# First queries of an attention + MoE kernel: order of loads, place of phi, and a mark for the second-layer weights

## The chip, the cores and the metric

One core of a Trainium2 chip. The metric is the device time of one execution in microseconds (us); lower is better.

## What is computed

Four batches of 576 tokens, 8 heads of 64. Causal attention is mixed with a read from a memory matrix, and the result goes through two matrix products with a gate between them:

```python
scores = where(causal, -1e9, q @ k.T / sqrt(D))
a = exp(scores - scores.max(-1)); a /= a.sum(-1) + 1e-09
local = a @ v
q_p = where(q > 0, q, exp(q) - 1) + 1            # phi
mem_out = (q_p @ M_prev) / (q_p . z_prev + 1e-06)
x = g * mem_out + (1 - g) * local                # g = sigmoid(beta)
h = x @ w_in                                     # 2304 x 512 by 512 x 2048
out = (h * sigmoid(1.702 * h)) @ w_out           # 2048 x 512
```

The weights arrive as 64-bit floating point and are rebuilt on the chip as 32-bit words.

## The kernel before

The work is tiled by pairs of heads: 4 batches times 4 pairs (`NP`) are 16 pairs, numbered 0 to 15. Tokens of a pair stand in blocks of 128 rows. A product with split operands (`mm` into `pm`) uses a high and a low part of each factor.

**First queries.** `first_queries(0)` computes the first 256 queries of batch 0, for all four pairs, before the planned part begins, so that the first tokens of x are there early. It loads the keys and queries of each pair (`fk`, L261 and L262, two loads each), the queries in rows (`fq`, L265), z (`fz`, L267), the values (`fv`, L269) and the memory (`fm`, L271), all on SP's queue. Then it goes through `score(c)` (products of L286 into a pair of PSUM tiles; VectorE masks and takes the maximum, L479, in place; ScalarE exponentiates, L485), `norm(c)` (sums, scaling, transposes L304 to L306, and the copies into `ft`, on ScalarE L136 and on VectorE L139), `phi` (Relu L314 and Exp L315 on ScalarE, then VectorE L316 and products with z on VectorE and GpSimd, and the scaling of the memory by ScalarE), `phin` (sums L325, reciprocal, scaling), `qtr(k)` (transposes of the queries, L339) and `values(c)` (L350), which adds memory and local part of a pair and splits the result into `xh` and `xl`. PSUM tiles come from `bank`, which hands out four tiles in turn.

**w_in.** 16 blocks of 128 columns. `conv_unit` loads a block of 64-bit words (`wraw`, 512 KB, L198 on SP's queue), ScalarE scales the upper words (`ws`, L206), VectorE puts the 32-bit word together in three steps (L213, L214, L216), ScalarE copies its high part and GpSimd subtracts to get the low part (`wi`). Two buffers for raw words serve the first six blocks (`W0`); later odd blocks have two of their own. The first six are written out behind `first_queries`, the others at the slots in `CONV`.

**Pairs.** `plan_prep` and `plan_attend` lay out the 16 pairs in numbered slots (`K0`, `at`), `first_moe` fills TensorE's remaining time with the first product of x, chunk by chunk (256 or 320 tokens of batch 0, 288 of the others). At the start of a pair's slots stands its tail: the last 64 rows of both heads, with `exp_tail` (ScalarE, tile `at`). Outputs of the pairs of a batch go out to memory (`xd<-xf`, L646) and come back as `xl` (L640 or L708). The first product's results are copied (`hk`) and stored (`gd`), to be loaded again for the second product.

**w_out.** `conv_pair(kk)` loads two blocks of raw words of the second-layer weights on GpSimd's queue (`load`, L847), then ScalarE (L851) and VectorE rebuild them. The calls stand behind the sixteen pairs in the program text. Where their buffers are free at the start, nothing in the program keeps the loads from being taken much earlier.

**Order.** Each engine works through its own list in order. The list is made by the framework: of the instructions whose inputs are there in its own plan, it takes the one that stands first in the program text (`tc.high_priority` moves a group ahead). `tc.add_manual_dep(x, y, NOSYNC)` only says that x comes behind y in that list; with `SYNC` the engine of x also waits for y. SP and GpSimd issue DMAs from their lists like any other instruction. The call order in `first_queries` is:

```python
score(0); phi(); score(1); norm(0); phin(); score(2); norm(1)
qtr(0); qtr(1); values(0, xl); score(3); norm(2)
values(1, xl); norm(3); values(2, xl); values(3, xl)
```

Of the kernel before, what the change touches and what calls it, by code (L numbers as in the profile page):

```python
# [16 lines left out]
NP = H // 2  # L17
# [17 lines left out]
def tile_attention_memory_moe(ctx, tc, kq, vq, mem, zz, beta, w_in, w_out, out):  # L35
# [157 lines left out]
    def conv_unit(slot, dst, src, rp, rkw, wp, wkw, sp, skw):  # L193
# [7 lines left out]
        def scale():  # L201
            if wp() is None:
                box["s"] = box["r"] = sp.tile([128, DM], F32, name="wr", **skw)
            else:
                box["s"] = wp().tile([128, DM], F32, name="ws", **wkw)
            nc.scalar.activation(  # L206
                out=box["s"], in_=box["raw"][:, :, 1].bitcast(F32), func=AF.Copy, scale=2.0 ** -112)

# [13 lines left out]
        if slot is None:  # L222
            for fn in parts:
                fn()
            return
# [26 lines left out]

    direct, done = set(), set()

    def first_queries(b):
# [3 lines left out]
        for c in range(NP):  # L259
# [3 lines left out]
            K.append(t)  # L263
        q = fst.tile([128, NP, 2, 128], F32, name="fq")
        nc.sync.dma_start(q, vq[b, :, :, 1, :2].rearrange("c p t d -> p c t d"))  # L265
        z = fst.tile([128, NP, 128], F32, name="fz")
        nc.sync.dma_start(z.rearrange("p c d -> p (c d)"), zz[b:b + 1].rearrange("o c d -> o (c d)").to_broadcast([128, NP * 128]))  # L267
        v = fst.tile([128, NP, 2, 128], F32, name="fv")
        nc.sync.dma_start(v, vq[b, :, :, 0, :2].rearrange("c p t d -> p c t d"))  # L269
        m = fst.tile([128, NP, 128], F32, name="fm")  # L270
        nc.sync.dma_start(m, mem[b * NP:b * NP + NP].rearrange("c p h d -> p c (h d)"))  # L271
# [9 lines left out]
        def score(c):  # L281
# [7 lines left out]
            for h in range(2):  # L289
                for i, (o, n) in enumerate(((256, 128), (0, 256))):  # L290
                    nm = softmax_max([(ps[h][:, o:o + n], n, mask[:, 512 - n:])])
                    softmax_exp(ps[h][:, o:o + n], aa[c][:, h, o:o + n], nm, fsm[c][:, h, i, :1])

        def norm(c):
# [13 lines left out]
            copy("A", fa[c][:, :512], pt[0])  # L308
            copy("V", fa[c][:, 512:], pt[1][:, :256])

        def phi():
            qv = q.rearrange("p c t (h d) -> p (c t) h d", h=2)
            w = qm[:, :, :, :D]
            nc.scalar.activation(out=w, in_=qv, func=AF.Relu, scale=-1.0)  # L314
            nc.scalar.activation(out=w, in_=w, func=AF.Exp, scale=-1.0)  # L315
            nc.vector.scalar_tensor_tensor(out=qv, in0=qv, scalar=0.0, in1=w, op0=ALU.max, op1=ALU.add)  # L316
            for c in range(NP):
                tt("VP"[c % 2], w[:, 2 * c:2 * c + 2], qv[:, 2 * c:2 * c + 2],
                   z[:, c:c + 1, :].rearrange("p o (h d) -> p o h d", h=2).to_broadcast([128, 2, 2, D]), ALU.mult)
                copy("A", m[:, c], m[:, c], gt[:, c:c + 1])  # L320
# [38 lines left out]
        phi()  # L359
        score(1)  # L360
        norm(0)
        phin()
        score(2)
        norm(1)
        qtr(0)
        qtr(1)
        values(0, xl)
        score(3)
# [4 lines left out]
        values(3, xl)  # L373

# [115 lines left out]
    def plan_attend(p):  # L490
# [63 lines left out]
        def exp_tail():  # L554
            U["at"] = wkp.tile([128, S], F32, name="at", bufs=2)
            U["st"] = tails[p % 2]
            for f in range(2):
                x = softmax_exp(U["ps"][f][:, :CH], U["at"][:, CH * f:CH * f + CH], U["nm"], U["st"][:, f:f + 1])
                used(U["ps"][f], x)

# [214 lines left out]

    def conv_in(blk):
        wb[blk] = w1[blk].tile([128, 2, DM], F32R, name=f"wi{blk}")
        other = blk >= W0 and blk % 2 == 1
        raw = (att, {"tag": "W1", "bufs": 2}) if other else (cnv, {"bufs": 2})
        ws = (lambda: ps_o, {"tag": "po"}) if other else (lambda: ps_x, {"tag": "ps"})  # L780
# [291 lines left out]
```

## Time and profile before

| | us |
|---|---|
| median of three runs | 641.17 |
| lowest and highest run | 640.54, 646.22 |
| profiled execution, its own time | 648.07 |
| span of the profiled execution (first to last instruction) | 646.3 |
| TensorE busy in the span | 602.6 |

The profile is of one execution. Its span is the time from the first to the last instruction. A row of a timeline gives start, duration, engine, line, operation and tiles, then in brackets how long the engine stood idle before and what released it ("<-"). Stretches give the busy time of each engine in a window with the number of instructions, the granted TensorE clock (1.00 is full speed), the mean share of the DMA engines and what they moved. The chain of waits is followed back from the last instruction: each piece is what ended last.

### The profile page before, as it was taken

Reading aid. Unit: us, or ns where it says so; the run is one execution under the profiler, and the core shown is the slowest. Engines: PE = TensorE matmul, PEld = TensorE weight load, DVE = VectorE, ACT = ScalarE, POOL = GpSimd, SP = SyncE. Lnnn points to the kernel's source line nnn. Section 1 sums busy time; section 2 is a strip of 40 time slices with the busy share of each in tenths; the row PEclk is TensorE's granted clock in tenths of the full one; section 3 lists DMA queues with packets and bytes.
Section 4 is the critical chain, followed back from the end, with each engine's and each line's share of the span. In section 5 each row is a group of like instructions: output and inputs, shape, how many; then the busy total and the mean of one; then the engine's idle time right before and its main releaser. Section 6 shows DMA issues by size and latency. Waiting matters only on the chain.

```text
span 646.3 us, 11501 instructions
## 1 busy us (share of the span) xinstructions
PE 602.6 (93%) x4000; PEld 522.7 (81%) x4000; DVE 414.3 (64%) x1015; ACT 363.0 (56%) x836; POOL 183.7 (28%) x253
## 2 busy tenths in 40 slices
PE   3698998999979999989999999899989999999997
PEld 2458765688657787778888889899989999999996
DVE  3998866654665445544455437889496579458944
ACT  4776575544564468354554335665876764776451
POOL 3556644532456433343544112310000000000000
PEclk9988999999999999999999999899999999999999
DMA  8848642323444155243342115775745630671002
GB/s 248 297 148 261 186 158 88 129 70 129 138 134 138 52 177 167 73 153 96 123 153 83 49 66 186 231 238 173 238 145 171 186 133 15 206 212 57 25 2 73
DMA packets 59370, 90.61 MB, mean 140 GB/s; under 512 B 5680, under 2 KB 48176, under 8 KB 59312
## 3 DMA queue, kind: packets, MB, share of 16 engines
q1 hardware_dynamic: 57008, 81.49, 40.1%
q0 software_dynamic: 2304, 8.39, 4.2%
q8 instruction: 31, 0.51, 0.3%
q14 instruction: 27, 0.22, 0.1%
HBM read 63.02 MB, written 26.84 MB: 139 GB/s over the span
## 4 chain that ended last, share of the span: by engine, by line
PE 66%; DMA 12%; ACT 9%; DVE 7%; issue 3%; SPq 1%; POOL 1%; DVEq 0%; ACTq 0%; POOLq 0%
PE acc L935 23%; PE pm L125 22%; PE po L125 7%; PE pt L131 7%; PE ps L125 7%; DMA gd<-hk 3%; DMA xl<-xd 3%; DMA xd<-xf 2%; DMA g<-gd 2%; ACT a L485 2%; DMA fq<-in_vq_dram 1%; DVE g L144 1%; ACT hk L136 1%; DMA qr<-in_vq_dram 1%; DVE ps L479 1%
## 5 line engine op out<-in xcount | busy, mean ns | idle before, releaser
L125 PE MATMUL pm<-xh,wi 128*128 128x288 f32 (+2 forms) x1024 | 219.4, 307 | 11.3 <-ACT hk L136 5.9
L125 PEld LDWEIGHTS pm<-xh,wi 128*128 128x128 f32 x1024 | 168.5, 194 | 14.9 <-ACT hk L136 7.0
L935 PE MATMUL acc<-oh,wo 128*128 128x384 f32 x672 | 158.3, 337 | 0.9 <-ACT oh L136 0.7
L125 PE MATMUL pm<-xl,wi 128*128 128x288 f32 (+2 forms) x512 | 154.3, 303 | 0.0
L935 PEld LDWEIGHTS acc<-oh,wo 128*128 128x128 f32 x672 | 120.0, 188 | 2.7 <-ACT oh L136 2.7
L144 DVE TENSOR_TENSOR ol<-g,oh 128x768 fp32r<-128x768 f32 x84 | 79.2, 955 | 49.0 <-ACT oh L136 44.4
L479 DVE CUSTOM_DVE_ANT_0 ps<-ps,mask 128x256 f32<-128x256 f32 (+4 forms) x144 | 67.5, 506 | 61.6 <-PE ps L125 54.8
L488 POOL TENSOR_SCALAR a<-a,sm,g 128x512 f32<-128x512 f32 (+3 forms) x112 | 71.6, 651 | 116.4 <-DVE sm L538 100.0
L935 PE MATMUL acc<-ol,wo 128*128 128x384 f32 x336 | 99.7, 339 | 2.7 <-DVE ol L144 2.6
L125 PEld LDWEIGHTS pm<-xl,wi 128*128 128x128 f32 x512 | 98.6, 193 | 1.1 <-DVE wr L216 1.1
L485 ACT ACTIVATE a<-ps,nm 128x256 f32<-128x256 f32 (+2 forms) x112 | 59.9, 542 | 63.9 <-DVE nm L479 63.1
L136 ACT ACTIVATE oh<-g 128x768 fp32r<-128x768 f32 x84 | 70.2, 840 | 42.3 <-PE acc L935 40.9
L125 PE MATMUL ps<-kqf 128*128 128x288 f32 (+4 forms) x288 | 67.9, 480 | 4.6 <-ACT at L485 2.3
L935 PEld LDWEIGHTS acc<-ol,wo 128*128 128x128 f32 x336 | 61.5, 188 | 5.3 <-DVE ol L144 5.3
L136 ACT ACTIVATE hk<-pm 128x288 f32<-128x288 f32 (+2 forms) x85 | 34.1, 410 | 38.2 <-PE pm L125 26.8
L131 PE MATMUL pt<-ident,a 128*128 128x128 f32 x296 | 53.2, 274 | 0.0
L898 ACT ACTIVATE g<-g 128x768 f32<-128x768 f32 x48 | 40.3, 844 | 20.3 <-DMA g<-gd 17.8
L125 PEld LDWEIGHTS po<-e,vr 128*64 128x64 f32 x416 | 29.9, 137 | 20.1
L131 PE MATMUL pt<-ident,at 128*128 128x128 f32 x160 | 41.4, 285 | 4.9 <-ACT a L485 3.5
L125 PE MATMUL po<-e,vr 128*64 128x320 f32 (+3 forms) x416 | 45.4, 359 | 0.0
L144 DVE TENSOR_TENSOR g<-g,g 128x768 f32<-128x768 f32 x48 | 44.1, 953 | 1.2 <-ACT g L898 1.1
L125 PEld LDWEIGHTS ps<-kqf 64*128 64x128 f32 (+1 forms) x288 | 30.1, 189 | 17.8 <-issue 7.4
(127 smaller groups left out, 751.5 us busy)
## 6 DMA issues: line engine op xcount, KB each, us to landing
g<-gd SPq DMA_DIRECT2D x48, 384.0 KB, 3.9
gd<-hk SPq DMA_DIRECT2D x96, 144.0 KB, 2.0
wraw<-in_w_out_dram POOLq DMA_DIRECT2D x16, 512.0 KB, 4.8
wraw<-in_w_in_dram SPq DMA_DIRECT2D x16, 512.0 KB, 4.8
kqf<-in_kq_dram SPq DMA_DIRECT2D x12, 608.0 KB, 6.6
vr<-in_vq_dram SPq DMA_DIRECT2D x16, 320.0 KB, 6.0
qr<-in_vq_dram SPq DMA_DIRECT2D x12, 320.0 KB, 3.2
xd<-xf SPq DMA_DIRECT2D x10, 288.0 KB, 6.4
```

Source lines behind the costliest of these rows:

```text
L125: x = nc.tensor.matmul(out, l, r, start=start, stop=stop)
L131: nc.tensor.transpose(out, in_, idn)
L136: return nc.scalar.activation(out=dst, in_=src, func=AF.Copy, **kw)
L144: (nc.vector if eng == "V" else nc.gpsimd).tensor_tensor(out=dst, in0=a, in1=b, op=op)
L479: nc.vector.tensor_tensor_reduce(out=ps, in0=ps, in1=mk, op0=ALU.add, op1=ALU.min, scale=-0.125, scalar=1e38 if j == 0 else nm[:, j - 1:j] ...
L485: return nc.scalar.activation(out=a, in_=ps, func=AF.Exp, scale=-1.0, bias=nm, accum_out=sm)
L488: (nc.vector if eng == "V" else nc.gpsimd).tensor_scalar(out=a, in0=a, scalar1=r, scalar2=gcol, op0=ALU.mult, op1=ALU.mult)
L898: nc.scalar.activation(out=t, in_=t, func=AF.Gelu_apprx_sigmoid)
L935: nc.tensor.matmul(acc[b, j][:, :QN], W[2 * p + kk][:, WPART[i], sp, 128 * j:128 * j + 128], mv[:, kk], start=first and p + kk == 0 and sp ...
```

## The change

In `first_queries` the loads go out as fk of pairs 0 and 1, fq, fk of pairs 2 and 3, fz, the raw words of w_in block 0, fm, fv. `phi` is called behind `norm(1)`, its Relu behind the ScalarE copy of `ft` of pair 0; the scaling of the memory stands behind the copy of `ft` of pair 1. `score(3)` is called ahead of `qtr` and `values`. The first scaling of w_in words stands behind the last exponential of `score(2)`. All these are orders of ScalarE's list, without a wait. The loads of w_out wait for the last exponential of the tail of the thirteenth pair (number 12). `conv_unit` hands back its five parts, so that the first load can be issued apart from the rest.

```diff
@@ -203,8 +203,11 @@
                 box["s"] = box["r"] = sp.tile([128, DM], F32, name="wr", **skw)
             else:
                 box["s"] = wp().tile([128, DM], F32, name="ws", **wkw)
-            nc.scalar.activation(
+            x = nc.scalar.activation(
                 out=box["s"], in_=box["raw"][:, :, 1].bitcast(F32), func=AF.Copy, scale=2.0 ** -112)
+            behind = state.pop("behind", None)
+            if behind is not None:
+                tc.add_manual_dep(x.ins, behind, NOSYNC, reason="raw words")
 
         def bits():
             raw, si = box["raw"], box["s"].bitcast(I32)
@@ -220,9 +223,7 @@
         parts = (load, scale, bits, lambda: copy("A", dst[:, 0], box["r"]),
                  lambda: sub("P", dst[:, 1], box["r"], dst[:, 0]))
         if slot is None:
-            for fn in parts:
-                fn()
-            return
+            return parts
         for k, prio, fn in zip((0, 2, 2, 3, 3), (5, 60, 61, 40, 41), parts):
             at(slot + k, prio, fn)
 
@@ -250,25 +251,41 @@
         copy("A", xh[:, c, :w], src)
         sub("V", xl[:, c, :w], src, xh[:, c, :w])
 
+
+    def conv_in(blk):
+        wb[blk] = w1[blk].tile([128, 2, DM], F32R, name=f"wi{blk}")
+        other = blk >= W0 and blk % 2 == 1
+        raw = (att, {"tag": "W1", "bufs": 2}) if other else (cnv, {"bufs": 2})
+        ws = (lambda: ps_o, {"tag": "po"}) if other else (lambda: ps_x, {"tag": "ps"})
+        return conv_unit(None, wb[blk], w_in[blk], *raw, *ws, att, {"tag": f"qpt{blk % 2}", "bufs": 2})
+
     direct, done = set(), set()
 
     def first_queries(b):
         K, fsm = [], []
         if b == 0:
             nc.sync.dma_start(gb, beta.to_broadcast([128, H]))
-        for c in range(NP):
+
+        def load_fk(c):
             t = fst.tile([128, 512], F32, name=f"fk{c}")
             nc.sync.dma_start(t[:, :256], kq[b, c, :, :256])
             nc.sync.dma_start(t[:, 256:], kq[b, c, :, S:S + 256])
             K.append(t)
+
+        load_fk(0)
+        load_fk(1)
         q = fst.tile([128, NP, 2, 128], F32, name="fq")
         nc.sync.dma_start(q, vq[b, :, :, 1, :2].rearrange("c p t d -> p c t d"))
+        load_fk(2)
+        load_fk(3)
         z = fst.tile([128, NP, 128], F32, name="fz")
         nc.sync.dma_start(z.rearrange("p c d -> p (c d)"), zz[b:b + 1].rearrange("o c d -> o (c d)").to_broadcast([128, NP * 128]))
+        parts = conv_in(0)
+        parts[0]()
+        m = fst.tile([128, NP, 128], F32, name="fm")
+        nc.sync.dma_start(m, mem[b * NP:b * NP + NP].rearrange("c p h d -> p c (h d)"))
         v = fst.tile([128, NP, 2, 128], F32, name="fv")
         nc.sync.dma_start(v, vq[b, :, :, 0, :2].rearrange("c p t d -> p c t d"))
-        m = fst.tile([128, NP, 128], F32, name="fm")
-        nc.sync.dma_start(m, mem[b * NP:b * NP + NP].rearrange("c p h d -> p c (h d)"))
         qm = fst.tile([128, NP * 2, 2, D + 1], F32, name="fqm")
         nc.gpsimd.memset(qm[:, :, :, D:], 1e-6)
         for c in range(NP):
@@ -289,7 +306,8 @@
             for h in range(2):
                 for i, (o, n) in enumerate(((256, 128), (0, 256))):
                     nm = softmax_max([(ps[h][:, o:o + n], n, mask[:, 512 - n:])])
-                    softmax_exp(ps[h][:, o:o + n], aa[c][:, h, o:o + n], nm, fsm[c][:, h, i, :1])
+                    x = softmax_exp(ps[h][:, o:o + n], aa[c][:, h, o:o + n], nm, fsm[c][:, h, i, :1])
+                    box["e", c] = x.ins.name
 
         def norm(c):
             sm = fst.tile([128, 2, 2], F32, name="fsr", bufs=2)
@@ -305,19 +323,21 @@
                 nc.tensor.transpose(pt[0][:, 256 * h + 128:256 * h + 256], aa[c][:, h, 0:128], ident)
                 nc.tensor.transpose(pt[1][:, 128 * h:128 * h + 128], aa[c][:, h, 128:256], ident)
             fa[c] = fst.tile([128, 768], F32, name="ft", bufs=2)
-            copy("A", fa[c][:, :512], pt[0])
+            box["f", c] = copy("A", fa[c][:, :512], pt[0]).ins.name
             copy("V", fa[c][:, 512:], pt[1][:, :256])
 
-        def phi():
+        def phi(behind):
             qv = q.rearrange("p c t (h d) -> p (c t) h d", h=2)
             w = qm[:, :, :, :D]
-            nc.scalar.activation(out=w, in_=qv, func=AF.Relu, scale=-1.0)
+            x = nc.scalar.activation(out=w, in_=qv, func=AF.Relu, scale=-1.0)
+            tc.add_manual_dep(x.ins, behind, NOSYNC, reason="phi")
             nc.scalar.activation(out=w, in_=w, func=AF.Exp, scale=-1.0)
             nc.vector.scalar_tensor_tensor(out=qv, in0=qv, scalar=0.0, in1=w, op0=ALU.max, op1=ALU.add)
             for c in range(NP):
                 tt("VP"[c % 2], w[:, 2 * c:2 * c + 2], qv[:, 2 * c:2 * c + 2],
                    z[:, c:c + 1, :].rearrange("p o (h d) -> p o h d", h=2).to_broadcast([128, 2, 2, D]), ALU.mult)
-                copy("A", m[:, c], m[:, c], gt[:, c:c + 1])
+                x = copy("A", m[:, c], m[:, c], gt[:, c:c + 1])
+                tc.add_manual_dep(x.ins, box["f", 1], NOSYNC, reason="memory")
 
         def phin():
             n = fst.tile([128, NP, 2, 2, 1], F32, name="fn")
@@ -356,21 +376,23 @@
         xl = new_x(b)
         xq[b][0] = mop.tile([128, NK, XW], F32R, name="xh")
         score(0)
-        phi()
         score(1)
         norm(0)
-        phin()
         score(2)
         norm(1)
+        phi(box["f", 0])
+        state["behind"] = box["e", 2]
+        phin()
+        score(3)
         qtr(0)
         qtr(1)
         values(0, xl)
-        score(3)
         norm(2)
         values(1, xl)
         norm(3)
         values(2, xl)
         values(3, xl)
+        return parts
 
 
     pairs = [(b, c) for b in range(B) for c in range(NP)]
@@ -557,6 +579,8 @@
             for f in range(2):
                 x = softmax_exp(U["ps"][f][:, :CH], U["at"][:, CH * f:CH * f + CH], U["nm"], U["st"][:, f:f + 1])
                 used(U["ps"][f], x)
+            if p == len(pairs) - 4:
+                state["mark"] = x.ins.name
 
         def inv_tail():
             st = U["rt"] = sml.tile([128, 1], F32, name="st")
@@ -772,20 +796,13 @@
                 break
 
     NPAIRS = len(pairs)
-
-    def conv_in(blk):
-        wb[blk] = w1[blk].tile([128, 2, DM], F32R, name=f"wi{blk}")
-        other = blk >= W0 and blk % 2 == 1
-        raw = (att, {"tag": "W1", "bufs": 2}) if other else (cnv, {"bufs": 2})
-        ws = (lambda: ps_o, {"tag": "po"}) if other else (lambda: ps_x, {"tag": "ps"})
-        conv_unit(None, wb[blk], w_in[blk], *raw, *ws, att, {"tag": f"qpt{blk % 2}", "bufs": 2})
-
     for b in range(MB):
-        first_queries(b)
+        parts = first_queries(b)
         xplan[b] = -7
         if b == 0:
             for blk in range(W0):
-                conv_in(blk)
+                for fn in (parts[1:] if blk == 0 else conv_in(blk)):
+                    fn()
     first.close()
     w1 += [pool(left, f"w1_{k}", side="left", reuse_waits="tile") for k in range(W0, NB)]
     load_kq(0)
@@ -794,7 +811,7 @@
         plan_prep(p)
         plan_attend(p)
     for blk in range(W0, NB):
-        at(CONV[blk - W0], 58, lambda blk=blk: conv_in(blk))
+        at(CONV[blk - W0], 58, lambda blk=blk: [fn() for fn in conv_in(blk)])
     fill["gen"] = first_moe()
     while state["slot"] < K0[-1] + 16:
         step()
@@ -844,7 +861,8 @@
 
         def load(h):
             box["raw", h] = (cnv, stg)[kk % 2].tile([128, DM, 2], I32, name="wraw", bufs=2)
-            nc.gpsimd.dma_start(box["raw", h].rearrange("p f w -> p (f w)"), w_out[kk + KK * h].bitcast(I32))
+            x = nc.gpsimd.dma_start(box["raw", h].rearrange("p f w -> p (f w)"), w_out[kk + KK * h].bitcast(I32))
+            tc.add_manual_dep(x.ins, state["mark"], SYNC, reason="not yet")
 
         def scale(h):
             box["s", h] = ps_w.tile([128, DM], F32, name="ws", tag="pm2")
```

## Rows read from the trace of the kernel before

**Rows 1.** The page: busy time of TensorE, and the chain's shares by engine.

```profile
PE 602.6 (93%) x4000; PEld 522.7 (81%) x4000; DVE 414.3 (64%) x1015; ACT 363.0 (56%) x836; POOL 183.7 (28%) x253
...
PE 66%; DMA 12%; ACT 9%; DVE 7%; issue 3%; SPq 1%; POOL 1%; DVEq 0%; ACTq 0%; POOLq 0%
```

**Rows 2.** Stretches: start:end length, busy PE, PEld, DVE, ACT, POOL; PEclk, DMA, GB/s.

```profile
8.00:15.00 7.00, 1.97 (x7) 1.28 (x7) 2.45 (x12) 3.12 (x13) 1.03 (x2) 1.00 1.03 313
15.00:28.00 13.00, 8.10 (x32) 6.04 (x34) 12.45 (x34) 9.62 (x27) 6.34 (x9) 1.00 1.00 364
28.00:44.00 16.00, 14.45 (x86) 8.02 (x84) 14.78 (x44) 11.59 (x32) 7.79 (x10) 0.97 0.42 128
44.00:54.00 10.00, 8.07 (x50) 7.03 (x47) 8.73 (x25) 6.25 (x14) 8.04 (x9) 0.84 0.79 263
54.00:76.00 22.00, 21.23 (x160) 19.70 (x158) 19.29 (x41) 14.72 (x35) 13.68 (x13) 0.94 0.71 214
280.00:292.00 12.00, 9.52 (x56) 8.16 (x55) 4.29 (x14) 4.17 (x13) 5.40 (x8) 0.86 0.37 113
```

**Rows 3.** Timeline of ScalarE (ACT), 6 to 20 us.

```profile
13.28 1.06 ACT L314 ACTIVATE fqm<-fq 128x1024 f32<-128x1024 f32 x1 [3.32 <-DMA fq<-in_vq_dram]
14.24 0.46 ACT L485 ACTIVATE fa<-ps,nm 128x256 f32<-128x256 f32 x1
...
17.48 1.28 ACT L136 ACTIVATE fm<-fm,gt 128x128 f32<-128x128 f32 x4 [0.45 <-DMA fm<-in_mem_dram]
...
19.00 0.61 ACT L206 ACTIVATE ws<-wraw 128x512 f32<-128x512 f32 x1
```

**Rows 4.** Timeline of VectorE (DVE), 6 to 20 us.

```profile
15.17 0.43 DVE L479 CUSTOM_DVE_ANT_0 ps<-ps,mask 128x256 f32<-128x256 f32 x1 [3.71 <-ACT fa L485]
```

**Rows 5.** The chain of waits, 0 to 80 us: start, duration, what.

```profile
4.97 8.28 DMA fq<-in_vq_dram
...
44.38 5.45 DMA wraw<-in_w_in_dram
...
52.94 4.63 PE pm L125 x24
...
65.12 3.02 PE pm L125 x23
```

**Rows 6.** DMA issues, 0 to 30 us: count, KB each, us to landing.

```profile
fk<-in_kq_dram SPq DMA_DIRECT2D x8, 128.0 KB, 3.1
wraw<-in_w_out_dram POOLq DMA_DIRECT2D x2, 512.0 KB, 6.9
...
fv<-in_vq_dram SPq DMA_DIRECT2D x1, 512.0 KB, 10.6
```

**Rows 7.** w_out's issues by count (min/median/max ns, first to last), and GpSimd's gap.

```profile
L847 POOL DMA_DIRECT2D wraw<-in_w_out_dram x4: 541/592/694, 3.9 to 74.0; - x4
...
L847 POOL DMA_DIRECT2D wraw<-in_w_out_dram x12: 530/530/607, 394.1 to 436.6; - x12
...
287.36 2.31 POOL L144 TENSOR_TENSOR xl<-xl,xh 128x288 fp32r<-128x288 f32 x3 [5.79 <-ACT xh L136]
```

**Rows 8.** Timeline of ScalarE: pair 12's tail, first use of w_out.

```profile
279.25 0.54 ACT L485 ACTIVATE at<-ps,nm 128x288 f32<-128x288 f32 x1
...
388.99 1.18 ACT L851 ACTIVATE ws<-wraw 128x512 f32<-128x512 f32 x2
```

**Rows 9.** Timeline of TensorE (PE), 4 to 36 us.

```profile
12.27 0.42 PE L306 MATMUL pt<-ident,fa 128*128 128x128 f32 x1
14.84 2.80 PE L286 MATMUL ps<-fk 64*128 64x256 f32 x8 [2.15 <-ACT fa L485]
...
28.70 1.09 PE L350 MATMUL po<-ft,fv 128*64 128x256 f32 x8
```

**Rows 10.** Chain of waits from 274 us on, and the load of x there.

```profile
276.37 6.54 DMA xd<-xf
...
xl<-xd SPq DMA_DIRECT2D x1, 432.0 KB, 3.9
```

## The prediction

> **What bounds the kernel now.** I read the page first: engine shares and the shares of the chain that ended last [rows 1]. TensorE is busy 602.6 us of 646.3, and 66% of the chain is its own. It stands idle for 43.7 us in all, and only there, or where it runs slowly, can a reordering gain. Next come the stretches [rows 2]: from 8 to 15 us TensorE works 1.97 us of 7, from 54 us on it is nearly full. What holds the time between is VectorE: 2.45 us of 7 up to 15 us, then 12.45 of 13, 14.78 of 16, 8.73 of 10 and 19.29 of 22, which is 55.25 of 61 us (91%). It normalises scores there, does phi's arithmetic, and rebuilds 16 blocks of w_in from 64-bit words. The DMA engines are full too, share 1.00 at 364 GB/s from 15 to 28 us.
>
> Third, the hole itself. ScalarE takes its list in order. Phi's Relu waits 3.32 us for fq, until 13.28 us, so since 9.96 us [rows 3]. Behind it stand the next exponentials of pair 1, the first of them starting at 14.24 us; VectorE, which must get the score tile back from them, stands idle for 3.71 us until 15.17 us [rows 4]. The chain of waits says the same: fq's 8.28 us of DMA comes early in it [rows 5]. fq is issued at 4.97 us, behind eight fk loads, and beside it run two w_out loads of 512 KB, from 3.9 us on [rows 5 to 7], although the first w_out block is converted at 388.99 us [rows 8].
>
> **The change part by part.** *Loads in the order of need.* fq moves ahead of four fk issues. Nine issues (gb and eight fk) take the queue to 4.97 us, so four are about 2 us, and fq goes out at about 3 us. Also 2 x 512 KB of w_out leave this stretch: 1.05 MB at 364 GB/s is 2.9 us of all the engines' time. I expect fq at 8 to 9 us in place of 13.25. The precise time hardly matters, for phi no longer stands where it is wanted so early.
>
> *phi behind the first copy of ft.* Relu, and with it Exp, go behind the ft copy of pair 0 on ScalarE, and the program text puts score(2) ahead. The pair-1 exponentials then run from about 10.5 us on. The transposes for ft end at 12.7 us [rows 9], so their copy can run right behind, and Relu at about 13.3 us. Even if fq landed as late as now (13.25 us), Relu would not wait. So the hole of 3.71 us closes: the products of score(2), which waited for ScalarE until 14.84 us, come behind the transposes at about 12.7 us [rows 9], and until its first scores VectorE has the ft copy, the sums and the scaling of norm(1). Gain: 3.7 us. Bounds: 3.3 us (the wait for fq alone) and 4.5 us, which is all that VectorE stands idle from 8 to 15 us (7 - 2.45 = 4.55 [rows 2]).
>
> What comes back: Relu (1.06 us, [rows 3]) and an Exp as long now stand among the exponentials of score(2). ScalarE works 9.62 of 13 us from 15 to 28 us [rows 2], so there is room, but an exponential can wait for one of them. Bounds 0 and 1.06 us; I take the middle, 0.5. phi's steps on VectorE stay what they are. They change places with scores, and on an engine that is 91% busy an exchange of places moves little.
>
> *score(3) ahead of the query transposes and values.* It brings the fourth part of x forward. Bounds: 0, because weights, not x, end the wait before 52.94 us (the w_in load of 44.38 us and its conversion [rows 5]), and 1.9 us, what TensorE is missing from 44 to 54 us [rows 2]. Nearest is the row of the weights, so I take 0.4.
>
> *w_in block 0 loaded earlier, fm ahead of fv, first conversion behind the exponentials of score(2).* fm was waited for 0.45 us at 17.48 us [rows 3]; it is now needed behind the second ft copy, so nothing. fv comes behind one more load of 512 KB (1.4 us at 364 GB/s). It lands 10.6 us after its issue [rows 6], near 17 us, and its first product starts at 28.70 us [rows 9]: over 11 us of cover; if that were gone, 1.4 us. The conversion of block 0 starts at 19.00 us now [rows 3]; the exponentials of score(2) should be over by 17 to 18 us, so the rule costs nothing (bounds: 1 us either way, as blocks come earlier or later). kqf, vr and the next w_in blocks stand behind the same bytes less 1.05 MB.
>
> *w_out from the thirteenth pair on.* Only four of the sixteen loads move, those between 3.9 and 74.0 us; the twelve from 394.1 us on have long passed their mark [rows 7]. The mark is the last exponential of pair 12's tail, at 279.25 us [rows 8]. POOL then stands idle for 5.79 us before 287.36 us [rows 7], and four issues of about 0.59 us (2.4 us) fit in. Queued behind them is POOL's part of the x split, which waits for xl anyway, and behind that TensorE; were the gap gone, 2.4 us would be paid. The first use at 388.99 us leaves some 100 us, over ten times the 6.9 us of the pair in [rows 6].
>
> But 2.1 MB move to an awkward place. The store of pair 11's output (276.37 us, 6.54 us) and the load of x from it (432 KB, right behind, landing after 3.9 us) hold up TensorE [rows 10], which is missing 2.5 us from 280 to 292 us at a mean clock of 0.86 [rows 2]. The DMA share there is 0.37, so more than half of the room is free. Bounds: 0 (the loads fall between), and 5.8 us (2.1 MB at 364 GB/s, all ahead of xl). Half a share while xl is in flight doubles the time of its 0.44 MB: 1.2 us. I take half of that, 0.6, as the place is open by some microseconds.
>
> The Trainium skill, "DMA: Bandwidth & Descriptors", section "Queues, rings and completion order", says that each DMA engine takes turns between the queues that have work, a packet at a time. The trace agrees: the first w_out pair landed after 6.9 us [rows 6], in which at 313 GB/s (8 to 15 us, [rows 2]) some 2.1 MB moved, twice its own. By that rule, the loads being in flight, the place near 283 us costs the 1.2 us, and the sum is 0.6 us smaller.
>
> Sum: -3.7 + 0.5 - 0.4 + 0.6 = -3.0 us. Against the profiled execution, whose 648.07 us are the span of 646.3 and 1.8 us around it that nothing here touches: 645.1 us. That execution stands 6.9 us (1.1%) above the median of the runs, 641.17 us; the same instructions run in both, so I take the 3.0 us from the median: 638.2 us.
>
> **The rivals.** *A, the other side: the w_out loads hold up x.* All four go out in POOL's gap before 287.36 us, ahead of the load of xl; TensorE waits 5.8 us more. With -3.6 us from the front that is +2.2 us: 643.4 us. It turns from gain to loss once xl is more than 3.6 us later. For it: time and place fit, and TensorE already waits there. Against it: the DMA engines are mostly idle there, and SP's queue keeps its own turn.
>
> *B, the front gives more.* VectorE is idle 4.55 us from 8 to 15 us, 0.55 from 15 to 28 and 1.22 from 28 to 44 us, 6.3 us in all. From 44 to 54 us TensorE's clock is 0.84 [rows 2], and 24 products from 52.94 us take 4.63 us, where 23 take 3.02 us soon after [rows 5]: 1.5 us. If x and weights come early and TensorE keeps its clock, 6.3 + 1.5 = 7.8 us are gained, less 0.6: 634.0 us. For it: the holes are there. Against it: the weights still arrive at VectorE's pace.
>
> *C, hidden anyway.* The 3.7 us are gained at 15 us and lost by 54 us: the load at 44.38 us takes 5.45 us [rows 5], and such loads wait for a free buffer, so for VectorE's last step on an earlier block. If the rebuilding of blocks is merely pushed behind the scores, the sixteenth block comes when it does now, and the time is 641.2 us, give or take 1. For it: VectorE at 91%. Against it: the work ahead of it is the same, and a hole of 3.71 us is gone. That the change doesn't do what it says (ScalarE's list waiting for fz or fk in fq's place) ends here too.
>
> **How the numbers follow.** Forecast 0.48, A 0.15, B 0.19, C 0.18. Differences of 1% (6.4 us) are about what a measurement of this kernel can tell from none; its three runs spread from 640.54 to 646.22 us. The forecast by itself reaches from 636 to 640.5 us (its terms' bounds, the middle one up to 2). Over the cases: 633.5 to 643.5 us. Faster by over 1%, below 634.8: most of B, 0.17. Slower by over 1%, above 647.6: the far end of A, where one late x delays the next, 0.06. Within 1%: 0.77.
>
> **What would show it.** Right: no wait of Relu for fq, no hole of VectorE from 12 to 15 us, the products of score(2) near 13 us, TensorE full some 3 us sooner than now; w_out loads near 280 us, and a wait for xl there longer by 0 to 1.2 us. Wrong: less than 2 us left at 76 us (C), over 3 us more of TensorE idle between 280 and 292 us (A), or a front shorter by over 6 us (B).

## The result, and the profile after

| | us |
|---|---|
| changed kernel, median of four runs (lowest, highest) | 653.88 (650.03, 654.12) |
| kernel before, beside it, median of four runs | 643.47 |
| ratio, 95% interval | 1.0125 [1.0086, 1.0164] |
| profiled execution after: its own time, its span | 654.1, 652.3 |

By the ratio, the change makes the kernel 1.25% slower, about 8 us. (The two medians are 10.4 us apart, more than that; the four runs of the kernel before alone spread over 5.7 us. What follows goes by the ratios.) The forecast was 3 us faster, and its range ended at 643.5 us. Between the two profiled executions the spans differ by 6.0 us (646.3 and 652.3).

The page of the changed kernel, its busy times and the chain's shares, answers to [rows 1]:

```profile
PE 599.7 (92%) x4000; PEld 519.2 (80%) x4000; DVE 415.3 (64%) x1015; ACT 363.9 (56%) x836; POOL 185.3 (28%) x253
...
PE 54%; DMA 19%; ACT 10%; DVE 10%; issue 5%; SPq 1%; POOL 1%; DVEq 0%; ACTq 0%; POOLq 0%
```

TensorE has the same 4000 instructions and is busy 2.9 us less, yet the span is 6.0 us longer: 8.9 us more of idling. Of the chain, DMA has 19% in place of 12%. Where that arose is read from the stretches, the same six as in [rows 2]:

```profile
8.00:15.00 7.00, 4.15 (x12) 2.70 (x13) 4.73 (x21) 3.60 (x16) 2.25 (x4) 1.00 1.01 304
15.00:28.00 13.00, 7.10 (x30) 5.79 (x28) 10.90 (x32) 9.86 (x31) 5.71 (x7) 1.00 0.72 259
28.00:44.00 16.00, 15.55 (x91) 8.87 (x91) 14.22 (x38) 11.08 (x27) 7.71 (x8) 1.00 0.39 129
44.00:54.00 10.00, 8.09 (x58) 6.85 (x57) 8.42 (x26) 7.71 (x19) 8.29 (x10) 1.00 0.80 241
54.00:76.00 22.00, 16.30 (x125) 14.67 (x124) 19.78 (x40) 13.17 (x29) 12.28 (x11) 1.00 0.60 195
280.00:292.00 12.00, 7.22 (x53) 6.07 (x51) 3.88 (x13) 1.96 (x7) 5.05 (x9) 0.94 0.88 306
```

Three things stand out. VectorE does 4.73 us from 8 to 15 us in place of 2.45, so most of the hole is filled; but from 15 to 28 us it does 10.90 in place of 12.45, and up to 54 us its four stretches add up to 38.27 us, where they were 38.41. TensorE then has only 16.30 of 22 us from 54 to 76 us, with 125 matrix instructions (21.23 us and 160 before). And from 280 to 292 us it has 7.22 of 12 (9.52 before) while the DMA share goes from 0.37 to 0.88.

The front, on ScalarE's timeline of the changed kernel (answers to [rows 3]):

```profile
14.25 0.60 ACT L136 ACTIVATE ft<-pt 128x512 f32<-128x512 f32 x1 [1.72 <-PE pt L323]
14.74 1.05 ACT L332 ACTIVATE fqm<-fq 128x1024 f32<-128x1024 f32 x1
...
16.03 1.06 ACT L334 ACTIVATE fqm<-fqm 128x1024 f32<-128x1024 f32 x1
...
20.12 0.48 ACT L507 ACTIVATE fa<-ps,nm 128x256 f32<-128x256 f32 x1
...
20.57 0.64 ACT L206 ACTIVATE ws<-wraw 128x512 f32<-128x512 f32 x1
```

Relu (now L332) waits for nothing: fq landed at 7.4 us. The first scaling of w_in words (L206) stands directly behind the last exponential of `score(2)` (20.12 us, the fourth of that pair) and starts at 20.57, where it started at 19.00. VectorE's timeline (answers to [rows 4]):

```profile
12.62 0.16 DVE L314 TENSOR_REDUCE fsr<-fsm 128x4 f32<-128x8 f32 x1 [0.70 <-ACT fa L507]
...
16.17 0.43 DVE L501 CUSTOM_DVE_ANT_0 ps<-ps,mask 128x256 f32<-128x256 f32 x1 [1.29 <-ACT fa L507]
...
17.51 0.42 DVE L139 COPY ft<-pt 128x256 f32<-128x256 f32 x1 [0.60 <-PE pt L324]
...
26.49 0.68 DVE L219 SCALAR_TENSOR_TENSOR wr<-wraw,ws 128x512 int32<-128x512 int32 x1
```

The one hole of 3.71 us has become three small ones (0.70, 1.29, 0.60 us). The last row is the last step of w_in's first block; in the kernel before it stood at 24.6 us. All sixteen in one group (first and last start), of the kernel before and then of the changed one:

```profile
L216 DVE SCALAR_TENSOR_TENSOR wr<-wraw,ws x16: 673/680/689, 24.6 to 73.1; 128x512 int32<-128x512 int32 x16
```

```profile
L219 DVE SCALAR_TENSOR_TENSOR wr<-wraw,ws x16: 677/678/689, 26.5 to 74.5; 128x512 int32<-128x512 int32 x16
```

The sixteenth block comes 1.4 us later than before. TensorE's waits for rebuilt weights (`wi`) from 54 to 76 us say who needs it (total, times, longest; before, then after):

```profile
PE pm L125 <- ACT wi L136: 0.3, 1, 0.3
```

```profile
PE pm L125 <- ACT wi L136: 5.4, 3, 3.1
```

The pair's scaling on GpSimd (tile `a`, 128x512) marks how far a kernel has come. Three of these rows, of the kernel before and then of the changed one:

```profile
89.25 1.68 POOL L488 TENSOR_SCALAR a<-a,sm,g 128x512 f32<-128x512 f32 x2 [2.57 <-DVE sm L538]
262.89 1.52 POOL L488 TENSOR_SCALAR a<-a,sm,g 128x512 f32<-128x512 f32 x2 [3.78 <-ACT hk L136]
290.47 1.52 POOL L488 TENSOR_SCALAR a<-a,sm,g 128x512 f32<-128x512 f32 x2 [0.81 <-DVE sm L538]
```

```profile
90.97 1.68 POOL L510 TENSOR_SCALAR a<-a,sm,g 128x512 f32<-128x512 f32 x2 [2.93 <-DVE sm L560]
264.57 1.52 POOL L510 TENSOR_SCALAR a<-a,sm,g 128x512 f32<-128x512 f32 x2 [3.78 <-ACT hk L136]
296.71 1.52 POOL L510 TENSOR_SCALAR a<-a,sm,g 128x512 f32<-128x512 f32 x2 [0.81 <-DVE sm L560]
```

The one near 90 us starts at 90.97 us in place of 89.25, and the one near 263 us at 264.57 in place of 262.89: the front has cost 1.7 us, and it stays so for 170 us. The next such row is at 296.71 in place of 290.47: 4.6 us more are lost in between (6.24 less the 1.68 before it). There the chain of waits of the changed kernel (answers to [rows 10]) and GpSimd's timeline (answers to [rows 7]) read:

```profile
277.72 6.57 DMA xd<-xf
...
284.30 8.75 DMA xl<-xd
...
294.52 3.12 PE pm L125 x12
```

```profile
282.05 2.33 POOL L864 DMA_DIRECT2D wraw<-in_w_out_dram  x4
...
293.59 2.30 POOL L144 TENSOR_TENSOR xl<-xl,xh 128x288 fp32r<-128x288 f32 x3 [8.36 <-ACT xh L136]
```

The four loads of w_out go out at 282.05 us; the load of x is issued 2.25 us behind the first of them and takes 8.75 us where it took 3.9. TensorE's timeline has the wait, first before, then after:

```profile
288.29 0.56 PE L125 MATMUL pm<-xh,wi 128*128 128x288 f32 x2 [2.44 <-ACT hk L136]
```

```profile
294.52 0.85 PE L125 MATMUL pm<-xh,wi 128*128 128x288 f32 x2 [7.30 <-ACT hk L136]
```

From 2.44 to 7.30 us: 4.9 us. So there are two losses, one in the front and a larger one near 285 us.

### The profile page after: what moved, and what is told of

It reads as the page before. It is cut to its first block, busy times and chain, and to the rows that moved or that the text cites. A ratio compares the mean times of both kernels' runs of the same rounds, so it can differ in the third digit from the quotient of the medians.

```text
span 652.3 us, 11494 instructions
## 1 busy us (share of the span) xinstructions
PE 599.7 (92%) x4000; PEld 519.2 (80%) x4000; DVE 415.3 (64%) x1015; ACT 363.9 (56%) x836; POOL 185.3 (28%) x253
## 4 chain that ended last, share of the span: by engine, by line
PE 54%; DMA 19%; ACT 10%; DVE 10%; issue 5%; SPq 1%; POOL 1%; DVEq 0%; ACTq 0%; POOLq 0%
PE pm L125 21%; PE acc L953 9%; PE po L125 8%; PE ps L125 7%; PE pt L131 7%; DMA g<-gd 6%; DMA gd<-hk 4%; DVE ol L144 3%; DMA xl<-xd 3%; DVE g L144 2%; ACT oh L136 2%; DMA xd<-xf 2%; ACT g L916 2%; ACT a L507 2%; DMA fv<-in_vq_dram 1%
## 5 line engine op out<-in xcount | busy, mean ns | idle before, releaser
L125 PE MATMUL pm<-xh,wi 128*128 128x288 f32 (+2 forms) x1024 | 217.0, 304 | 20.4 <-ACT hk L136 11.5
L125 PEld LDWEIGHTS pm<-xh,wi 128*128 128x128 f32 x1024 | 165.5, 191 | 24.7 <-ACT hk L136 12.7
L125 PE MATMUL pm<-xl,wi 128*128 128x288 f32 (+2 forms) x512 | 152.4, 300 | 0.0
L510 POOL TENSOR_SCALAR a<-a,sm,g 128x512 f32<-128x512 f32 (+3 forms) x112 | 71.6, 653 | 117.1 <-DVE sm L560 101.5
L125 PEld LDWEIGHTS pm<-xl,wi 128*128 128x128 f32 x512 | 96.9, 190 | 0.5 <-DVE qp L456 0.5
L125 PEld LDWEIGHTS po<-e,vr 128*64 128x64 f32 x416 | 29.9, 137 | 20.2
L136 ACT ACTIVATE e<-pt 128x320 f32<-128x320 f32 (+2 forms) x76 | 32.8, 436 | 19.6 <-PE pt L131 16.4
```

Source lines behind the costliest of these rows:

```text
L125: x = nc.tensor.matmul(out, l, r, start=start, stop=stop)
L136: return nc.scalar.activation(out=dst, in_=src, func=AF.Copy, **kw)
L510: (nc.vector if eng == "V" else nc.gpsimd).tensor_scalar(out=a, in0=a, scalar1=r, scalar2=gcol, op0=ALU.mult, op1=ALU.mult)
```

## The experiments

Each run was compared with the kernel before on the same chip. The first block, the sixteenth block (last VectorE step, tile `wr`), the pair near 90 us (GpSimd's scaling) and the load of xl near 284 us with TensorE's wait behind it are from the traces, in us. A row of these is one execution, a ratio is many; differences between two ratios carry the width of both intervals.

| run | ratio, 95% interval | blocks 1 / 16 | pair near 90 | xl / wait |
|---|---|---|---|---|
| before | 1 | 24.6 / 73.1 | 89.25 | 3.9 / 2.44 |
| after | 1.0125 [1.0086, 1.0164] | 26.5 / 74.5 | 90.97 | 8.7 / 7.30 |
| e1: before + mark | 1.0116 [1.008, 1.0152] | 22.6 / 74.1 | 90.41 | 8.8 / 7.26 |
| e2: after - mark | 1.0044 [1.0023, 1.0065] | 27.6 / 74.5 | 90.95 | 4.1 / 2.71 |
| e3: after, later mark | 1.0048 [1.0016, 1.0079] | 26.5 / 74.3 | 90.42 | 4.0 / 2.76 |
| e4: before + later mark | 1.0028 [1.0002, 1.0054] | 22.1 / 74.4 | 90.57 | 4.1 / 2.73 |
| e12: after, two loads later | 1.0084 [1.0055, 1.0112] | 26.5 / 74.2 | 90.36 | 5.5 / 4.20 |
| e9: e3 - rule | 0.9983 [0.9951, 1.0015] | 15.2 / 70.7 | 87.19 | 4.0 / 2.49 |
| e13: after - rule | 1.0059 [1.0027, 1.0091] | 16.5 / 71.6 | 88.05 | 9.4 / 8.07 |
| e14: after - mark - rule | 1.0002 [0.9975, 1.0028] | 18.5 / 75.0 | 91.23 | 4.0 / 2.36 |
| e15: before + rule | 1.0039 [1.0009, 1.007] | 27.3 / 74.7 | 91.69 | 3.9 / 2.51 |
| e10: before + load order | 1.0002 [0.9963, 1.0041] | 20.2 / 72.4 | 89.09 | 4.1 / 2.57 |
| e11: before + call order | 1.0045 [1.0014, 1.0075] | 23.4 / 75.4 | 91.59 | 4.0 / 2.42 |

The "mark" is the wait of w_out's loads for the last exponential of pair 12's tail. The "rule" is that the first scaling of w_in words stands behind the last exponential of `score(2)`.

**e1, e2: the mark and the front, each alone.** e1 is the kernel before with the two parts of the diff that make the mark:

```diff
+            if p == len(pairs) - 4:
+                state["mark"] = x.ins.name
...
-            nc.gpsimd.dma_start(box["raw", h]...
+            x = nc.gpsimd.dma_start(box["raw", h]...
+            tc.add_manual_dep(x.ins, state["mark"], SYNC, reason="not yet")
```

> The kernel before with one part of the change alone: the w_out loads wait for the tail of the thirteenth pair. Theory 1 (two causes: the four loads delay x near 284 us by 4.9 us, and the reordered front gives nothing): xl lands after 8 to 9 us there, TensorE's wait behind it is about 7 us in place of 2.4, and the time is 3 to 5 us above before, less what the front gains from 1 MB less (0 to 2 us). Theory 2 (the loss comes from the front's new order, and the wait for x is made up later): within 2 us of before.

e2 is the changed kernel without these lines:

> The changed kernel without the mark: the w_out loads go where the lists put them (two near 4 us, two near 70 us), all else of the change stays. Theory 1: xl near 284 us lands after about 3.9 us again, TensorE's wait there is 2 to 3 us, and the time is 4 to 6 us below after, so 0 to 3 us above before. Theory 2: the time stays within 2 us of after.

e1 has nearly the whole loss by itself, with xl at 8.8 us; e2 has no loss near 284 us and is still 0.44% slower. The mark is most of it, and the front, which was to bring the gain, brings a loss. In e1 the pair near 90 us is already 1.2 us late: taking w_out's loads out of the front brought the first block forward by 2.0 us and the sixteenth back by 1.0. No run shows why.

**e3, e4: the same loads some 10 us later.** The mark is set on a later exponential of pair 12, behind the load of xl, in the changed kernel (e3) and in the kernel before (e4):

```diff
+            if p == len(pairs) - 4 and h == 1 and i == 3:
+                state["mark"] = x.ins.name
...
-            if p == len(pairs) - 4:
-                state["mark"] = x.ins.name
```

> The changed kernel with the mark on a later exponential of the same pair, so that GpSimd issues the four loads behind its part of the split of x; TensorE's and ScalarE's lists are the same as in after, VectorE's differ little. Theory 1: xl lands after 3.9 to 4.5 us, TensorE's wait there is 2 to 3 us, and the time falls by 4 to 5 us against after. Theory 2 (the wait is made up later, or the new lists cost it): within 1.5 us of after. The issues themselves (2.3 us on GpSimd ahead of the scaling of a) may give back up to 1 us.

> The kernel before with the later mark alone: no w_out load in the front, none beside the load of x, the front in its old order. Theory 1: no delay near 284 us, and what 1 MB less in the front is worth: 0 to 3 us below before. Theory 2: within 1 us of before.

GpSimd's timeline of e3 has the four issues behind the x split, not ahead of it:

```profile
288.67 2.31 POOL L144 TENSOR_TENSOR xl<-xl,xh 128x288 fp32r<-128x288 f32 x3 [6.13 <-ACT xh L136]
291.52 2.32 POOL L864 DMA_DIRECT2D wraw<-in_w_out_dram  x4 [0.54 <-ACT a L507]
293.88 1.51 POOL L510 TENSOR_SCALAR a<-a,sm,g 128x512 f32<-128x512 f32 x2
```

The load of xl is back at 4.0 us and the wait at 2.76 us. The ratios fall by 0.77% (after to e3) and 0.88% (e1 to e4), some 5 to 5.7 us; in the traces the wait falls by 4.5 us in both. Only the moment of the loads differs, and in the changed kernel their issues on GpSimd are over long before xl lands, so the bytes near 284 us are shown to be the cause. Of what is left of e4's loss (0.28%, 1.8 us), 1.3 us already stand at the pair near 90 us (90.57 for 89.25), as in e1.

**e12: half the bytes.** Of each pair of loads, one keeps the first mark and one gets the later one:

```diff
-            tc.add_manual_dep(x.ins, state["mark"], SYNC, reason="not yet")
+            tc.add_manual_dep(x.ins, state[("mark", "later")[h]], SYNC, reason="not yet")
```

> The changed kernel with two of the four w_out loads on the first mark and two on the later one. If the load of x is held up by the bytes issued ahead of it, half of them hold it up half as long: xl lands after 6 to 6.8 us (8.7 with four, 4.0 with none), TensorE's wait is about 5 us (7.3 and 2.8), and the time lies between after and e3_mark_later. If two loads in flight are enough to take the same share of the engines for as long as x needs, xl lands after 7.5 us or more.

xl takes 5.5 us, the wait is 4.20 us and the ratio stands between the two, though its interval overlaps both. The wait follows the bytes that are in flight, but not in proportion: the first half adds 1.4 us (2.76 to 4.20), the second 3.1. In e12 the two early loads are issued at 280.35 us, 2.35 us ahead of xl, so much of them is gone when xl comes: its queue's first packets move 2.0 us behind its issue, where they do 1.0 us behind it in the kernel before and 4.0 us in the changed one.

**e5, e6: a fourth buffer for `hk`.** From 54 to 76 us ScalarE's copy into `hk` waits for a store of `gd` to free its buffer, 2.1 us in the kernel before and 3.6 us in the changed one. A rival for the front's loss was that wait, so `hk` gets a fourth buffer, in e3 (e5) and in the kernel before (e6):

```diff
-            h = mop.tile([128, XW], F32, name="hk", bufs=3)
+            h = mop.tile([128, XW], F32, name="hk", bufs=4)
```

> The changed kernel with the later mark (as e3_mark_later) and four buffers for hk in place of three. In after, ScalarE stood 3.9 us waiting for stores of hk, with copies of rebuilt w_in blocks behind it. Theory H (these waits pace the blocks at the end of the front): the sixteenth block's last VectorE step comes 2 to 4 us before 74.4 us and the time falls by 2 to 4 us against e3_mark_later. Theory V (VectorE's work on the blocks paces them, so it matters little who waits): the step within 1 us of 74.4, the time within 1.5 us of e3_mark_later.

> The kernel before with four buffers for hk. ScalarE waited 2.1 us for a store of hk in its front. Theory H: sixteenth block up to 2 us before 73.1 us, time 1 to 3 us below before. Theory V: within 1 us of before.

The sixteenth block comes 0.8 us earlier in e5 than in e3 and 1.1 us earlier in e6 than in the kernel before, the wait is gone, and the time gains nothing: 1.006 [1.004, 1.0081] and 1.0063 [1.0032, 1.0094]. For these two kernels this rival falls. (Why e6 is slower, although its pair near 90 us comes at 88.14 us, 1.1 us earlier, stays open.)

**e7, e8: less work on VectorE.** Both leave out the left shift, one of the three steps that put a w_in word together, for all blocks (e7 from the kernel before, e8 from e3):

```diff
-            nc.vector.tensor_scalar(out=si, in0=si, scalar1=3, scalar2=None, op0=ALU.logical_shift_left)
```

> The kernel before without the first of VectorE's three steps on each w_in block (the left shift): 16 x 0.70 = 11.2 us less of VectorE's work in the first 76 us. It leaves out part of the rebuilding of w_in, so its time is that of a front with less VectorE work. Theory V: the sixteenth block comes 5 to 8 us before 73.1 us and the pairs behind it follow by 3 to 7 us. Theory H: blocks are held by loads and waits, so less than 2 us earlier.

> The changed kernel with the later mark, and the left shift of the w_in blocks left out in the same way. Theory V: the sixteenth block comes 5 to 8 us before 74.4 us; and if the blocks were all that ate the gain of the new front, this kernel is now up to 3 us ahead of e7_before_noshift at the pairs near 90 us. Theory H: less than 2 us earlier than e3_mark_later, and not ahead of e7_before_noshift.

Sixteen steps of 0.7 us are 11 us. The sixteenth block comes at 65.0 us (e7, 8.1 earlier) and 62.6 us (e8, 11.7 earlier), the pair near 90 us at 84.2 and 83.8 us, and the ratios are 0.9922 [0.9896, 0.9948] and 0.9924 [0.9899, 0.9948]. So VectorE's work on the blocks is on the path to the end of the front. With a third of the steps gone the two fronts are equal (0.9922 and 0.9924), which fits that the changed front's loss, too, hangs on when these steps are done; that is argued, not shown.

**e9: without the rule.** From e3 one line goes:

```diff
-        state["behind"] = box["e", 2]
```

> The changed kernel with the later mark (as e3_mark_later), without the rule that puts the first scaling of w_in words behind the last exponential of score(2). Theory P (the front's end is paced by VectorE's 91%, wherever the first block stands): the first block's last step comes 1 to 4 us before 26.5 us, the sixteenth within 1 us of 74.3 us, the time within 1.5 us of e3_mark_later. Theory Q (the late first block is what ate the gain): the sixteenth block and the pairs behind it 1.5 to 3 us earlier.

ScalarE's timeline of e9:

```profile
12.47 0.62 ACT L206 ACTIVATE ws<-wraw 128x512 f32<-128x512 f32 x1 [2.54 <-DMA wraw<-in_w_in_dram]
13.02 0.46 ACT L506 ACTIVATE fa<-ps,nm 128x256 f32<-128x256 f32 x1
...
17.90 0.62 ACT L206 ACTIVATE ws<-wraw 128x512 f32<-128x512 f32 x1
```

The first scaling is at 12.47 us (20.57 in the changed kernel), the second at 17.90 us (28.00). It costs what the rule was there to avoid: ScalarE waits 2.54 us for the raw words, and the exponential at 13.02 us stands behind it. But the first block is ready at 15.2 us in place of 26.5, the sixteenth 3.6 us earlier, the pair near 90 us 3.2 us earlier, and the ratio falls by 0.65%, about 4.2 us. With the loads of w_out out of the front, the rule was the loss there.

**e10, e11: load order alone, call order alone.** e10 is the kernel before with the new order of loads (without the mark); e11 has the call order with the places of phi and of the memory's scaling, the old order of loads, no rule and no mark. Their diffs are the corresponding parts of the change; the call order of e11:

```diff
         score(0)
-        phi()
         score(1)
         norm(0)
-        phin()
         score(2)
         norm(1)
+        phi(box["f", 0])
+        phin()
+        score(3)
         qtr(0)
...
-        score(3)
```

> The kernel before with the loads of the first queries in the new order and nothing else. Relu still stands ahead of the exponentials, but fq is issued at 3.1 us, not 4.97 us, and should land at 9 to 11 us. VectorE's hole of 3.71 us shrinks to 1 to 2.5 us. Theory P: sixteenth block within 1 us of 73.1 us, time within 1.5 us of before. Theory Q: what the hole gives is kept where the first block isn't held back, so 1.5 to 3 us below before.

> The kernel before with the new order of calls and the rules for phi and the memory, loads in the old order, no rule for w_in words, no mark. VectorE's hole at 15 us is gone or under 1.5 us. Theory P: sixteenth block within 1.5 us of 73.1 us and time 0 to 3 us above before, as in e2_front_only. Theory Q: 1.5 to 3 us below before.

e10 alone fills most of the hole: Relu still waits for fq, but only until 7.30 us (13.28 before), VectorE's longest hole is 2.30 us, and it does 5.04 us from 8 to 15 us. That was worth nothing at the end: 1.0002 [0.9963, 1.0041]. Two stretches of e10's trace say where it went:

```profile
8.00:54.00 46.00, 34.69 (x194) 24.38 (x194) 40.55 (x121) 32.98 (x93) 24.41 (x29) 1.00 0.72 251
54.00:76.00 22.00, 18.55 (x133) 16.91 (x132) 18.10 (x37) 12.68 (x28) 13.74 (x14) 0.92 0.65 201
```

VectorE has done 40.55 us by 54 us, 2.1 more than before (38.42), and TensorE 34.69, also 2.1 more (32.59). From 54 to 76 us TensorE then does 18.55 where it did 21.23: what was gained in front is handed back before 76 us. e11 fills it as well (4.73 us) and loses 0.45%: with phi's arithmetic moved behind and w_in's words loaded as late as before, the sixteenth block comes at 75.4 us. Why by so much stays open.

**e13, e14, e15: do the causes add, and is the rule enough?** Three runs asked whether the two causes are independent: the changed kernel without the rule (e13), without rule and mark (e14), and the kernel before with the rule alone (e15, the diff's lines for `behind` and for `box["e", c]`, with `state["behind"] = box["e", 2]` behind `norm(1)`).

> The change as it is, without the rule that puts the first scaling of w_in words behind the last exponential of score(2). Theory that the two causes add (the rule in the front, the mark in the middle): first block near 15 us in place of 26.5, sixteenth block and the pair near 90 us 3 to 4 us earlier than in the changed kernel (near 71 and 87.3 us), the load of xl still near 8.7 us with 7.3 us of wait on TensorE, and a time some 0.65% below the changed kernel's, 1.006 of the kernel before. Rival, that a gain in front is given back at the late load of xl: pair near 90 us earlier as above, but the pair near 290 us as in the changed kernel (296.7), ratio near 1.012.

> The changed front without the rule, and the loads of w_out without a mark, so in the front as in the kernel before. Theory that rule and mark are the whole loss: sixteenth block near 69 to 71 us, pair near 90 us at 87 to 88 us, load of xl near 4 us, ratio 0.994 to 0.998, faster than both kernels. Rival, that taking w_out's 1.05 MB out of the first 15 us is what makes the gain of the run with the later mark: blocks as in the kernel before, ratio 1.000 to 1.004.

> The kernel before with the rule alone. Theory that the rule alone makes the front's loss: first block at 26 us or later in place of 24.6, sixteenth block 1 to 3 us later than in the kernel before, ratio 1.002 to 1.005. Rival, that the rule costs only together with the new call order (score(2) and the ft copies ahead of phi): sixteenth block within 0.5 us of the kernel before, ratio 0.998 to 1.001.

Within the intervals they add. With rule and mark the ratio is 1.0125, with the mark alone 1.0059, with the rule (and the later mark) 1.0048, with neither (the later mark) 0.9983. The early mark costs 0.77% against the later one with the rule and 0.76% without it, the rule 0.66% with the first mark and 0.65% with the later one. In e13's profile the chain shows the late load once more:

```profile
275.14 6.60 DMA xd<-xf
...
281.76 9.45 DMA xl<-xd
```

e15 confirms that the rule by itself costs: 0.39%, the pair near 90 us 2.4 us later. e14 missed its forecast: the front without rule and mark isn't faster than the kernel before (1.0002), and its sixteenth block comes at 75.0 us, where e13's comes at 71.6. Its trace has a wait that e13's has not, ScalarE's for stores of `gd` from 54 to 76 us:

```profile
ACT hk L136 <- DMA gd<-hk: 6.9, 3, 3.1
```

That is the rival of e5 and e6 again. Of the w_out loads that e14 leaves in the front, two are issued at 3.9 us and the others at 69.8 and 75.9 us, when most of that wait is over; whether the first two lead to it isn't shown, and the ratios of e14 and e9 overlap. No kernel here that does the whole computation is measurably faster than the one before; the nearest is e9.

Two readings hold over the whole table. The pair near 90 us comes 16 to 17 us behind the sixteenth block in every row, so that block is what ends the front; but neither the first block nor VectorE's work done by 54 us decides it (e1 has done 40.21 us and e14 39.87, over 1.4 us more than the kernel before, and both have their sixteenth block later). And a trace's front doesn't always go with the time: e14 is 0.42% faster than e2, the same kernel with the rule, though its pair near 90 us comes 0.3 us later. That the rule costs time is shown four times (e9, e13, e14, e15); by which waits, only in part.

## Why the prediction was wrong

*The hole of 3.7 us.* What it said up to 15 us was right: no wait of Relu, the hole of 3.71 us gone, the rest of pair 1's exponentials from 10.49 us on (forecast 10.5), Relu at 14.74 us (forecast 13.3). The step from there failed: the 3.7 us were counted as time at the end. e10 has 2.6 us more of VectorE's work done by 15 us and a ratio of 1.0002, and e9, the best front, 0.9983: 1.1 us, with 0 inside its interval. That is rival C, to which the prediction gave 0.18, "gained at 15 us and lost by 54 us": by 54 us VectorE had done 38.27 us of work after, 38.41 before. In e10, which has 40.55 us by then, it is lost between 54 and 76 us; what takes it back there stays open.

*"The rule costs nothing."* This step failed too. It rested on the exponentials of `score(2)` being over by 17 to 18 us; the last of them began at 20.12 us. But the larger mistake was to price a place in ScalarE's list by the first conversion's start (1.6 us later than before) rather than by what it could have been: the raw words had been loaded earlier, and without the rule the first scaling runs at 12.47 us. The bound given was 1 us either way; e9 against e3 measures 3.6 us at the sixteenth block and 0.65%, 4.2 us, at the end.

*Relu among the exponentials (0.5 us) and `score(3)` ahead (-0.4 us).* Neither was measured alone. e11, which has both without the rule, lost 0.45%, so with the old order of loads they are no gain together.

*w_out near 283 us: 0.6 us.* The place, the gap on GpSimd and the 2.3 us of issues were as forecast (2.4); the size was wrong by a factor of eight, and this is the largest failure. The term was half of 1.2 us, which in turn gave xl half a share of the DMA engines from its issue on. The DMA queues while xl was in flight (packets, MB, share of 16 engines' time in the window; q0 is GpSimd's queue, q1 is SP's), of the kernel before from 282.9 to 287 us and of the changed one from 284 to 293.1:

```profile
q1 hardware_dynamic: 677, 0.73, 65.6%
```

```profile
q0 software_dynamic: 554, 2.01, 62.3%
q1 hardware_dynamic: 680, 0.73, 23.0%
```

The same 0.73 MB needed 4.1 us before and 9.1 us now. The sum over 9.1 us hides an order. Cut at 288 us, from xl's issue (284.30) on, the window has two parts that differ:

```profile
q0 software_dynamic: 342, 1.27, 93.2%
```

```profile
q1 hardware_dynamic: 680, 0.73, 41.0%
q0 software_dynamic: 201, 0.69, 37.9%
```

For 3.7 us w_out's queue had the engines to itself, and SP's moved nothing, though in the kernel before its first packets move about 1 us behind xl's issue. Only with the last third of w_out's bytes did the two run side by side. So xl began 3 us later and then took 1.9 us longer: 4.9 us of wait, and e1 and e13 show the same order (there, too, SP's queue moves nothing for 3.7 us). That is rival A's mechanism, w_out "all ahead of xl", for most of the bytes, and its 5.8 us are near. The prediction gave A a chance of 0.15 with the argument that "SP's queue keeps its own turn"; for 3.7 us it had none.

The Trainium skill, "DMA: Bandwidth & Descriptors", section "Queues, rings and completion order", has each DMA engine take turns between the queues a packet at a time. In the front of the kernel before, a stretch of the trace agrees: from 7.5 to 9.5 us 157 packets of GpSimd's queue stand beside 146 of SP's, though with 0.57 and 0.14 MB, for equal turns are not equal bytes where packets differ in size. Near 284 us the trace doesn't agree: no packet of SP's queue in 3.7 us, then 680 beside 201. No run shows why; the half share of the bytes that the prediction took held only from 288 us on.

*The sum.* In ratios: mark 0.77% (after to e3), rule 0.65% (e3 to e9), the rest -0.17% (e9) make 1.25%. These are steps of one path from the changed kernel to the one before, so they must add up to it; that the parts hardly depend on each other is what e13 shows. The forecast had -3.0 us; here the front without the rule is -1.1 us (not clear of 0), the rule +4.2 and the mark +5.0, together +8.1 us.

## What to carry to other kernels

Before counting a closed hole as gain, name what ends its stage, and ask whether that is now done sooner; here it was the sixteenth rebuilt block of weights, which a filled hole did not bring forward enough, and a rule of order that held the first step of the rebuilding back cost more than the hole could give. A transfer moved to where the DMA engines are idle is priced by the small transfer that somebody waits for there: allow for the whole of what was issued ahead of it, not for a share, cut the time in flight into pieces before reading shares from it, and place the mark behind that small transfer's landing, not ahead of its issue.

## What the runs showed of the hardware

Two queues in flight at once did not share the DMA engines evenly. xl was issued 2.25 us behind the first of w_out's four loads; in its first 3.7 us GpSimd's queue moved 1.27 MB with 93.2% of the engines' time and SP's nothing, and only then did both move, 0.73 MB in 680 packets of SP's beside 0.69 MB in 201 of GpSimd's. A load of 432 KB took 3.9 us with none of w_out's loads in flight, 5.5 us beside two of 512 KB and 8.7 us beside four.
